# Attention into a bilinear FFN on one core: the ring of attention outputs 2048 columns long instead of 2304

## The chip, the core and the metric

The kernel runs on one core of a Trainium2 chip. The metric is the device time of one execution in microseconds; a lower number is better. The core's engines are called as the profile calls them: PE is TensorE (matmuls; PEld are its weight loads), DVE is VectorE, ACT is ScalarE, POOL is GpSimd and SP is SyncE. They run side by side, each through its own list of instructions in order, and wait for one another through semaphores.

## What is computed

The reference is a sparse attention, whose output is the input of a bilinear feed-forward layer:

```python
batch, n_heads, seq, head_dim = (8, 8, 576, 64)
...
scores = scale * np.matmul(q, k.transpose(0, 1, 3, 2))
mask_local = (rel >= 0) & (rel < stride)                                  # heads 0 to 3, stride 32
mask_strided = (rel >= 0) & (pos[None, :] % stride == pos[:, None] % stride)   # heads 4 to 7
...
attn = attn / (np.sum(attn, axis=-1, keepdims=True) + 1e-09)
...
x = np.ascontiguousarray(attn_out.transpose(0, 2, 1, 3)).reshape(B * S, H * D)   # 4608 x 512
a = x @ w_a          # 512 x 1536
b = x @ w_b          # 512 x 1536
return (a * b @ w_out).astype(np.float32)     # 4608 x 512
```

## The kernel before

**The two halves and what joins them.** There are 8 batches of 576 tokens, 4608 tokens in all. The attention works by batch, the feed-forward layer by tiles of 512 tokens (TTOK), nine of them (0 to 8). They are joined by `xT`, a bf16 tile of 128 partitions, 4 blocks of 128 channels (KD), and a ring of columns, one for each token. The ring is XR = 4 batches, 2304 columns long. Token n lies in column n mod 2304.

**Writing the ring.** For batches 0 and 1 ScalarE copies transposed blocks into it (X_e). For batches 2 to 7 `step_VT` does it. A batch has eight units u = 0 to 7: channel block c = u // 2, half = u % 2; blocks 0 and 1 hold the local heads, 2 and 3 the strided ones. One unit is: S (scores into a PSUM tile `st`, Exp on ScalarE, L391, and the mask on VectorE, L401), and some slots later V. V is matmuls into the PSUM tile `o` (L484), ScalarE's Ln and Exp of the sums (L493, L494), which give their reciprocal, and two VectorE products of `o` with it, one for each head j, into partitions 0 to 63 and 64 to 127 of `xT` (L498 for local heads, L500 for strided). A local half is 288 tokens in a row. A strided half is 4 tokens of each 8 of the whole batch. There is one buffer of `o`, so the matmuls of V wait for the products of the V before.

**Reading the ring.** `ab_mm` (L578) computes the projections of a tile: 12 blocks f of 128 hidden channels, for each of the two weights 4 matmuls of 512 columns, one for each channel block, into one PSUM bank. Tile 4 holds tokens 2048 to 2559, which lie in columns 2048 to 2303 and 0 to 255. So its matmuls are cut in two, of 256 columns each, by the list `cuts`; every piece loads its weights again. ScalarE copies bank a into `a_sb` (L595), VectorE multiplies it with bank b into `pf` (L598; L600 in tiles 0 and 1).

**The second product.** Tiles 2 to 8 (FAST_Y) compute it by seven half-size products, in the order 3, 4, 1, 7, 5, 2, 6 (L683). Their operands are sums of parts of `pf`, which VectorE makes as `ps` (fast_s: L611, L613, L615). VectorE also adds some of the products' banks (L659, L662, L664, L672), ScalarE copies others, GpSimd subtracts (listed under L874), and SP stores the result.

**The order of the work.** It is written out by hand. A tile is 16 slots, 12 of projections and 4 of the second product. The dictionary LATER puts the units of batch b at positions counted from slot 16(b - 1): V0 at 1, V1 at 3, V2 at 5, V3 at 7, V4 at 9, V5 at 11, V6 at 12.5, V7 at 14. So batch b is written during tile b - 1: batch 3 during tile 2, batch 7 during tile 6. In the same slots VectorE transposes the q and k of later batches (L326, L331), which POOL's queue has loaded, and SP's queue moves the transposed blocks. L929 is a one-element GpSimd instruction that keeps POOL's queue in step with the slots.

Of the kernel before, what the change touches and what calls it, by code (L numbers as in the profile page):

```python
# [8 lines left out]
BF16 = mybir.dt.bfloat16  # L9
# [7 lines left out]
RS = 8  # L17
NP = 72
# [12 lines left out]
def kernel(  # L31
# [10 lines left out]
    nc = tc.nc  # L42
    B, H, S, D = q.shape
# [5 lines left out]
    KD = d_model // 128  # L49
    FD = d_ff // 128  # L50
    TTOK = 512
    NT = n_tok // TTOK
    HL = H // 2
    W = S // 2

    const = ctx.enter_context(tc.tile_pool(name="const", bufs=1))
# [97 lines left out]
                             rhs=nc.const_aps.tensor(1.0, [128, 224], BF16), start=True, stop=True)  # L154

    cur = {}
    XR = 4
    xT = const.tile([128, KD, XR * S], BF16)
    wa_sb = wp.tile([128, KD, d_ff], BF16)
    wb_sb = wp.tile([128, KD, d_ff], BF16)  # L160
    wo_sb = wp.tile([128, FD, d_model], BF16)
# [200 lines left out]
    def unit(u):  # L362

        c, half = u // 2, u % 2
        return (c, half, 128, LW, 3) if c < 2 else (c, half, NP, NP, 4)
# [85 lines left out]
    def V_n(b, u):  # L451
        c, half, M, n, G = unit(u)
        ov, _ = held.pop((b, "o", u))
        rc = held.pop((b, "rc", u))
        if (b, c // 2) not in xn:
            x = sb.tile([128, RS * 4 * D], BF16, tag="xr", name="xr", bufs=2)
            xn[b, c // 2] = x[:n, :S // n * 4 * D].rearrange("p (g h d) -> p g h d", h=4, d=D)
        x = xn[b, c // 2][:, :, 2 * (c % 2):2 * (c % 2) + 2, :]
        if c < 2 or b >= FIRST_D:
            dst = x[:, G * half:G * half + G].rearrange("p g j d -> p j g d")  # L460
        else:
            dst = x[:, :, half, :].rearrange("p (g j) d -> p j g d", j=2)
        nc.vector.tensor_mul(dst, ov, rc[:n, :, :G].unsqueeze(3).to_broadcast([n, 2, G, D]))

    def step_V(b, u):
        if b >= FIRST_D:
            step_VT(b, u)
            return
        V_p(b, u)
        V_r(b, u)  # L470
        V_n(b, u)

    def step_VT(b, u):

        c, half, M, n, G = unit(u)
        p = ps.pop((b, u))
        o = psum4["o"].tile([128, 2, 512], F32, tag="o", name="o")
        for i in range(G):
            for j in range(2):
                if c < 2:  # L480
                    vt = vl_buf[b % 2][:, (2 * c + j) * 6 + 3 * half + i]
                else:
                    vt = vs_buf[b % 2][:, 2 * (c - 2) + j, 4 * half + i]
                nc.tensor.matmul(o[:, j, i * n:(i + 1) * n], lhsT=vt, rhs=p[:M, j, i * n:(i + 1) * n], start=True, stop=True)  # L484

        r = sb.tile([128, RS * 4 * D], BF16, tag="xr", name="xr", bufs=2)[:64, :4 * W].bitcast(F32)
        r = r.rearrange("p (j w) -> p j w", j=2)
        if c < 2:
            sums = o[64:, :, :W]
        else:  # L490

            sums, r = (t.rearrange(e, p=NP) for t, e in ((o[64:, :, :W], "d j (g p) -> d j p g"), (r, "d j (p g) -> d j p g")))
        nc.scalar.activation(r, sums, ACT.Ln)  # L493
        nc.scalar.activation(r, r, ACT.Exp, scale=-1.0)  # L494
        for j in range(2):
            dst = xT[64 * j:64 * j + 64, c, S * (b % XR):S * (b % XR + 1)]
            if c < 2:
                nc.vector.tensor_mul(dst[:, W * half:W * (half + 1)], o[:64, j, :W], r[:, j])  # L498
            else:
                nc.vector.tensor_mul(dst.rearrange("d (p r) -> d p r", r=RS)[:, :, G * half:G * (half + 1)],  # L500
                                     o[:64, j, :W].rearrange("d (g p) -> d p g", p=NP), r[:, j])

    def X_p(b, c):
        x = xn[b, c // 2][:, :, 2 * (c % 2):2 * (c % 2) + 2, :]
# [7 lines left out]
    def X_e(b, c):  # L512
        n = LW if c < 2 else NP
        tp = held.pop((b, "x", c))
        tv = tp.rearrange("d (g p) -> d g p", p=n)
        dst = xT[:, c, S * (b % XR):S * (b % XR + 1)]
        if c >= 2:
            dst, tv = dst.rearrange("d (p r) -> d p r", r=RS), tv.rearrange("d g p -> d p g")
        else:
            tv = tp  # L520
        nc.scalar.copy(dst, tv)

    def step_X(b, c):
        X_p(b, c)
        X_e(b, c)

    PART = {"Tkp": lambda c: T_p(0, c, "k"), "Tke": lambda c: T_e(0, c, "k"), "Tqp": lambda c: T_p(0, c, "q"),
            "Tqe": lambda c: T_e(0, c, "q"), "Sp": lambda u: S_p(0, u), "Sx": lambda u: S_x(0, u),
            "Sm": lambda u: S_m(0, u), "Vp": lambda u: V_p(0, u), "Vr": lambda u: V_r(0, u), "Vn": lambda u: V_n(0, u),
            "Xp": lambda c: X_p(0, c), "Xe": lambda c: X_e(0, c)}  # L530

    ORDER = """
# [34 lines left out]
        return psum4[nm].tile(shape, F32, tag=nm, name="mm")  # L567

    def ab_mm(t, f, ab, kks, mid=None, first=0, last=KD - 1):
        n = min(TTOK, XR * S - TTOK * t % (XR * S))  # L570
        cuts = [(0, n)] + ([(n, TTOK - n)] if n < TTOK else [])
        for w, ps_ in zip((wa_sb, wb_sb), ab):
            if mid and ps_ is ab[1]:
                mid()
            for kk in kks:
                for c0, n in cuts:
                    x0 = (TTOK * t + c0) % (XR * S)
                    nc.tensor.matmul(ps_[:, c0:c0 + n], lhsT=w[:, kk, 128 * f:128 * (f + 1)], rhs=xT[:, kk, x0:x0 + n],  # L578
                                     start=(kk == first and c0 == 0), stop=(kk == last and c0 == cuts[-1][0]))

    def ffn_ab(t, f, mid, ab=None):
        if f == 0:
            pfs[t] = fsb.tile([128, FD, TTOK], BF16, tag="pf", name="pf", bufs=1)
        pf = pfs[t]
        if ab is None:
            ab = [mm_bank([128, TTOK]) for _ in range(2)]
            if f == 0:

                late = 1 if t == 1 else 3
                ab_mm(t, f, ab, [kk for kk in range(KD) if kk != late], last=-1)  # L590
                ab_mm(t, f, ab, [late], first=-1, last=late)
            else:
                ab_mm(t, f, ab, range(KD), mid)
        a_sb = fsb.tile([128, TTOK], F32, tag="a_sb", name="a_sb")
        nc.scalar.copy(a_sb, ab[0])  # L595
        if t in FAST_Y:
            halves = lambda x: x.rearrange("p (a i s) -> p a i s", i=2, s=16)
            nc.vector.tensor_mul(pf[:, f, :].rearrange("p (i a s) -> p a i s", i=2, s=16), halves(a_sb), halves(ab[1]))  # L598
        else:
            nc.vector.tensor_mul(pf[:, f, :], a_sb, ab[1])  # L600
        return pf[:1, f, :1]
# [192 lines left out]
    with tc.manual_schedule(engines={ENG.PE, ENG.SP, ENG.Pool, ENG.DVE, ENG.Activation}):  # L794
# [28 lines left out]
        first = {}  # L823
        for nm in ORDER:
            if nm[0] == "*":
                spin(int(nm[1:]))
            elif nm == "C0":
                for x, cp, n in ((raw[0], nc.vector.tensor_copy, "k"), (raw[1], nc.scalar.copy, "q")):
                    t = nats[0, n, False][:, 0:2].rearrange("p h r d -> p (h r d)")
# [21 lines left out]
            elif nm[0] == "F":  # L851
                f = int(nm[1])
# [110 lines left out]
```

## Time and profile before

| | |
|---|---|
| median of the runs shown | 329.73 us (329.67 to 330.11, 4 runs) |
| the profiled execution, its own time | 329.77 us |
| its span (first to last instruction) | 327.6 us |
| granted TensorE clock, mean of the span | 0.998 |
| projections, L578, 512 columns | 727 matmuls in the record, 379 ns each from start to end |
| projections, L578, 256 columns (tile 4) | 192 matmuls, 273 ns each |
| weight loads of the projections, L578 | 960, 98 ns each |
| products into the ring, L498 | 48 of 64 x 288, 447 ns each |
| products into the ring, L500 | 48 of 64 x 288, 448 ns each |

A row of the profile's groups names the line, the engine and the operation, the tile written and the tiles read, the shape, the number of instructions, the busy time in us and the mean of one in ns. In the timeline a row begins with the start and the duration in us; neighbours of one kind are merged ("x4"), and the duration then goes from the first start to the last end. The matmuls are pipelined: one begins before the one ahead has ended, so their pace is the distance of the starts. Some records of matmuls are missing (727 of 768 of the first kind are there).

### The profile page before, as it was taken

Reading aid. Unit: us, or ns where it says so; the run is one execution under the profiler, and the core shown is the slowest. Engines: PE = TensorE matmul, PEld = TensorE weight load, DVE = VectorE, ACT = ScalarE, POOL = GpSimd, SP = SyncE. Lnnn points to the kernel's source line nnn. Section 1 sums busy time; section 2 is a strip of 40 time slices with the busy share of each in tenths; the row PEclk is TensorE's granted clock in tenths of the full one; section 3 lists DMA queues with packets and bytes.
Section 4 is the critical chain, followed back from the end, with each engine's and each line's share of the span. In section 5 each row is a group of like instructions: output and inputs, shape, how many; then the busy total and the mean of one; then the engine's idle time right before and its main releaser. Section 6 shows DMA issues by size and latency. Waiting matters only on the chain.

```text
span 327.6 us, 7651 instructions
## 1 busy us (share of the span) xinstructions
PE 320.7 (98%) x2793; PEld 206.0 (63%) x2824; DVE 265.5 (81%) x509; ACT 201.1 (61%) x325; POOL 177.2 (54%) x296
## 2 busy tenths in 40 slices
PE   8999999999999999999999999999999999999995
PEld 6754555455555577557999985559555954584474
DVE  6767787889777999999999999999877945647662
ACT  5763676468777775876577757776777543313321
POOL 8945938887956665775577557844312131232021
PEclk9999999999999999999999999999999999999999
DMA  9999999799999599899998999898024022004004
GB/s 155 145 204 201 204 184 184 159 180 120 140 205 114 96 94 82 75 211 132 79 87 169 159 88 75 143 204 85 20 63 128 2 67 64 0 2 128 1 2 128
DMA packets 98870, 37.50 MB, mean 114 GB/s; under 512 B 76689, under 2 KB 96017, under 8 KB 98833
## 3 DMA queue, kind: packets, MB, share of 16 engines
q0 software_dynamic: 85968, 19.48, 66.5%
q1 hardware_dynamic: 12576, 17.34, 18.3%
q8 instruction: 22, 0.36, 0.4%
q10 hardware_dynamic: 288, 0.20, 0.2%
q14 instruction: 16, 0.12, 0.1%
HBM read 39.51 MB, written 9.44 MB: 149 GB/s over the span
## 4 chain that ended last, share of the span: by engine, by line
PE 88%; DMA 4%; POOL 4%; issue 1%; DVE 1%; ACT 0%; POOLq 0%; DVEq 0%
PE mm L578 53%; PE mm L683 17%; PE mm L765 6%; PE st L383 4%; DMA wb_sb<-in_moe_w_b_dram 4%; PE o L484 4%; PE mm L711 2%; POOL shared L196 1%; POOL vl L224 1%; POOL wa_sb L251 1%; PE end L711 1%; PE o L440 0%; POOL wb_sb L251 0%; POOL tk L237 0%; PE tp L509 0%
## 5 line engine op out<-in xcount | busy, mean ns | idle before, releaser
L578 PE MATMUL mm<-xT,wb_sb 128*128 128x512 bf16 (+1 forms) x468 | 109.6, 358 | 0.2
L578 PE MATMUL mm<-xT,wa_sb 128*128 128x512 bf16 (+1 forms) x451 | 108.8, 357 | 1.0
L595 ACT COPY a_sb<-mm 128x512 f32<-128x512 f32 x106 | 62.0, 585 | 49.1 <-PE mm L578 47.8
L929 POOL CAST pace<-pf 1x1 f32<-1x1 bf16 x84 | 31.3, 372 | 83.8 <-DVE pf L598 81.0
L578 PEld LDWEIGHTS <-wb_sb 128*128 128x128 bf16 x480 | 46.1, 98 | 44.9 <-DMA wb_sb<-in_moe_w_b_dram 1.2
L598 DVE TENSOR_TENSOR pf<-a_sb,mm 128x512 bf16<-128x512 f32 x84 | 56.4, 671 | 17.0 <-PE mm L578 13.8
L578 PEld LDWEIGHTS <-wa_sb 128*128 128x128 bf16 x480 | 42.6, 98 | 31.4
L391 ACT ACTIVATE p<-st 128x576 bf16<-128x576 f32 (+1 forms) x64 | 41.5, 649 | 12.8 <-PE st L383 11.9
L493 ACT ACTIVATE xr<-o 64x576 f32<-64x576 f32 x48 | 31.1, 647 | 25.1 <-PE o L484 24.2
L683 PEld LDWEIGHTS <-ps 128*128 128x128 bf16 x360 | 34.6, 98 | 3.9
L494 ACT ACTIVATE xr<-xr 64x576 f32<-64x576 f32 x48 | 32.8, 683 | 1.5
L498 DVE TENSOR_TENSOR xT<-o,xr 64x288 bf16<-64x288 f32 x48 | 21.5, 447 | 7.7 <-ACT xr L494 7.1
L500 DVE TENSOR_TENSOR xT<-o,xr 64x288 bf16<-64x288 f32 x48 | 21.5, 448 | 6.4 <-ACT xr L494 5.1
L683 PE MATMUL mm<-wf,ps 128*128 128x256 bf16 x216 | 26.4, 273 | 0.0
L401 DVE TENSOR_TENSOR p<-p,mask_l 128x576 int16<-128x576 int16 x32 | 22.2, 692 | 1.3 <-ACT p L391 1.3
L765 PE MATMUL mm<-wo_sb,pf 128*128 128x512 bf16 x91 | 22.8, 379 | 0.3
L242 POOL DMA_DIRECT2D vs<-in_v_dram x24 | 19.6, 818 | 3.4 <-PE st L383 2.2
L600 DVE TENSOR_TENSOR pf<-a_sb,mm 128x512 bf16<-128x512 f32 x22 | 14.8, 673 | 5.3 <-ACT a_sb L595 3.7
L211 POOL DMA_DIRECT2D ql<-in_q_dram x24 | 16.0, 666 | 5.2 <-DMA wo_sb<-in_moe_w_out_dram 4.1
L211 POOL DMA_DIRECT2D kl<-in_k_dram x24 | 16.1, 671 | 4.8 <-issue 4.0
L929 POOL COPY pace<-y_sb 1x1 f32<-1x1 f32 x16 | 2.8, 175 | 28.8 <-ACT y_sb L666 15.0
L683 PE MATMUL mm<-wf,pf 128*128 128x256 bf16 x144 | 17.6, 273 | 0.0
(160 smaller groups left out, 503.8 us busy)
## 6 DMA issues: line engine op xcount, KB each, us to landing
out_dram<-y_sb SPq DMA_DIRECT2D x12, 512.0 KB, 4.8
out_dram<-y_sb SPq DMA_DIRECT2D x10, 256.0 KB, 3.7
vl<-in_v_dram POOLq DMA_DIRECT2D x6, 384.0 KB, 6.9
kl<-in_k_dram POOLq DMA_DIRECT2D x24, 72.0 KB, 3.1
ql<-in_q_dram POOLq DMA_DIRECT2D x24, 72.0 KB, 3.3
vs<-in_v_dram POOLq DMA_DIRECT2D x24, 72.0 KB, 4.0
wo_sb<-in_moe_w_out_dram POOLq DMA_DIRECT2D x4, 384.0 KB, 9.1
natk<-in_k_dram POOLq DMA_DIRECT2D x20, 72.0 KB, 3.4
```

Source lines behind the costliest of these rows:

```text
L211: nc.gpsimd.dma_start(out=t[32 * h:32 * h + 32], in_=src[b, h].rearrange("(i y) d -> y i d", y=32))
L391: nc.scalar.activation(p[:M, :, :W], st[:M, :, :W], ACT.Exp, scale=scale)
L401: nc.vector.tensor_tensor(pi, pi, mk, op=ALU.bitwise_and)
L493: nc.scalar.activation(r, sums, ACT.Ln)
L494: nc.scalar.activation(r, r, ACT.Exp, scale=-1.0)
L498: nc.vector.tensor_mul(dst[:, W * half:W * (half + 1)], o[:64, j, :W], r[:, j])
L578: nc.tensor.matmul(ps_[:, c0:c0 + n], lhsT=w[:, kk, 128 * f:128 * (f + 1)], rhs=xT[:, kk, x0:x0 + n], start=(kk == first and c0 == 0), sto ...
L595: nc.scalar.copy(a_sb, ab[0])
L598: nc.vector.tensor_mul(pf[:, f, :].rearrange("p (i a s) -> p a i s", i=2, s=16), halves(a_sb), halves(ab[1]))
L683: nc.tensor.matmul(bank[b][:, q], lhsT=lhs(g, q), rhs=rhs(g), start=new and q == 0 and g == 0, stop=g == FG - 1, skip_group_check=True)
L765: nc.tensor.matmul(ybank[j], lhsT=pf[:, f, 128 * j:128 * (j + 1)], rhs=wo_sb[:, f], start=(f == 0), stop=(f == FD - 1))
L929: nc.gpsimd.tensor_copy(pace, done)
```

## The change

The ring becomes XC = 4 x 512 = 2048 columns long. A tile's 512 tokens now always lie in one piece, so `ab_mm` loses its cuts, and tile 4 reads columns 0 to 511. Batches 3 (tokens 1728 to 2303) and 7 (tokens 4032 to 4607) now run over the end of the ring. The new function `x_parts` gives one or two pieces (column, first token, end token), and `step_VT` writes each with an instruction of its own; a strided half is cut along its positions. X_e writes batches 0 and 1 to the same columns as before.

```diff
-    XR = 4
-    xT = const.tile([128, KD, XR * S], BF16)
+    XC = 4 * TTOK
+    xT = const.tile([128, KD, XC], BF16)
...
+    def x_parts(b, t0, t1):
+        x0 = (S * b + t0) % XC
+        e = t0 + XC - x0
+        return ((x0, t0, e), (0, e, t1)) if e < t1 else ((x0, t0, t1),)
...
         for j in range(2):
-            dst = xT[64 * j:64 * j + 64, c, S * (b % XR):S * (b % XR + 1)]
+            x = xT[64 * j:64 * j + 64, c]
             if c < 2:
-                nc.vector.tensor_mul(dst[:, W * half:W * (half + 1)], o[:64, j, :W], r[:, j])
+                for x0, t0, t1 in x_parts(b, W * half, W * (half + 1)):
+                    nc.vector.tensor_mul(x[:, x0:x0 + t1 - t0], o[:64, j, t0 - W * half:t1 - W * half],
+                                         r[:, j, t0 - W * half:t1 - W * half])
             else:
-                nc.vector.tensor_mul(dst.rearrange("d (p r) -> d p r", r=RS)[:, :, G * half:G * (half + 1)],
-                                     o[:64, j, :W].rearrange("d (g p) -> d p g", p=NP), r[:, j])
+                for x0, t0, t1 in x_parts(b, 0, S):
+                    ps_ = slice(t0 // RS, t1 // RS)
+                    dst = x[:, x0:x0 + t1 - t0].rearrange("d (p r) -> d p r", r=RS)
+                    nc.vector.tensor_mul(dst[:, :, G * half:G * (half + 1)],
+                                         o[:64, j, :W].rearrange("d (g p) -> d p g", p=NP)[:, ps_], r[:, j, ps_])
...
-        dst = xT[:, c, S * (b % XR):S * (b % XR + 1)]
+        dst = xT[:, c, S * b:S * (b + 1)]
...
-        n = min(TTOK, XR * S - TTOK * t % (XR * S))
-        cuts = [(0, n)] + ([(n, TTOK - n)] if n < TTOK else [])
+        x0 = TTOK * t % XC
         for w, ps_ in zip((wa_sb, wb_sb), ab):
             if mid and ps_ is ab[1]:
                 mid()
             for kk in kks:
-                for c0, n in cuts:
-                    x0 = (TTOK * t + c0) % (XR * S)
-                    nc.tensor.matmul(ps_[:, c0:c0 + n], lhsT=w[:, kk, 128 * f:128 * (f + 1)], rhs=xT[:, kk, x0:x0 + n],
-                                     start=(kk == first and c0 == 0), stop=(kk == last and c0 == cuts[-1][0]))
+                nc.tensor.matmul(ps_, lhsT=w[:, kk, 128 * f:128 * (f + 1)], rhs=xT[:, kk, x0:x0 + TTOK],
+                                 start=kk == first, stop=kk == last)
```

## The prediction, made before the changed kernel was run

> **What bounds the kernel now.** I read the page first, then a table of the tiles, then TensorE's and VectorE's timelines around the places that the change touches. All durations are of the one profiled execution: 329.77 us, of which its span is 327.6 and 2.17 lies around it. The median of the runs shown is 329.73, so what is added to 329.77 can be added to the median.
>
> ```profile
> PE 320.7 (98%) x2793; PEld 206.0 (63%) x2824; DVE 265.5 (81%) x509; ACT 201.1 (61%) x325; POOL 177.2 (54%) x296
> ...
> PE 88%; DMA 4%; POOL 4%; issue 1%; DVE 1%; ACT 0%; POOLq 0%; DVEq 0%
> ```
>
> TensorE is busy 98% of the span and carries 88% of the chain that ended last. The clock row of the page is 9 in every slice. So a microsecond taken from TensorE's stream counts in full, provided that nobody else is late. The busy times of five tiles (2 to 6, each cut from its first projection to that of the next) say who could be:
>
> ```profile
> core 0: us, PE busy (x) PEld busy (x) DVE busy (x) ACT busy (x) POOL busy (x), PEclk, DMA share, GB/s
> 93.69:127.71 34.03, 33.87 (x293) 21.70 (x294) 30.93 (x57) 25.01 (x41) 20.07 (x36) 1.00 0.95 117
> 127.71:161.74 34.02, 33.81 (x292) 21.70 (x294) 33.51 (x58) 24.52 (x39) 22.92 (x39) 1.00 0.98 125
> 161.74:196.00 34.27, 34.27 (x392) 31.09 (x390) 33.39 (x57) 24.51 (x39) 22.74 (x38) 1.00 0.95 123
> 196.00:230.03 34.02, 33.82 (x292) 21.70 (x294) 33.29 (x57) 24.52 (x39) 21.40 (x37) 1.00 0.96 123
> 230.03:263.80 33.77, 33.56 (x286) 21.45 (x288) 27.60 (x51) 24.51 (x39) 6.98 (x12) 1.00 0.18 52
> ```
>
> Tile 4 (third row) has some 100 matmuls more than its neighbours, yet lasts only 0.24 us longer. VectorE is nearly full in tiles 2 to 5 and has room only in tile 6. No wait of TensorE is listed in any of these tiles: both engines are full, and TensorE leads by a little.
>
> **What goes: tile 4's second pieces.** Each of its 24 groups (12 blocks, two weights) is 8 matmuls of 256 columns now and becomes 4 of 512. TensorE's timeline shows one group of each kind; a group's pace is the distance to the next group's start:
>
> ```profile
> 133.66 1.03 PE L578 MATMUL mm<-xT,wa_sb 128*128 128x512 bf16 x4
> 134.52 1.03 PE L578 MATMUL mm<-xT,wb_sb 128*128 128x512 bf16 x4
> ...
> 167.74 1.04 PE L578 MATMUL mm<-xT,wa_sb 128*128 128x256 bf16 x8
> 168.61 1.04 PE L578 MATMUL mm<-xT,wb_sb 128*128 128x256 bf16 x8
> ```
>
> That is 0.86 us whole and 0.87 cut. By single starts in the trace the steps are 215.6 ns and 109.2 ns, so a group saves 8 x 109.2 - 4 x 215.6 = 11 ns, and 24 groups 0.27 us. The tile table, which contains everything else too, gives 34.27 - 34.02 = 0.24 (34.266 against 34.025 by starts). I take **-0.24**. The 96 weight loads that go too last 98 ns each, but lie beside the matmuls: they are worth nothing by themselves. Even if all of it is won, the kernel is 0.07% faster.
>
> **What comes: VectorE parts.** Batch 3 occupies ring columns 1728 to 2304, so it is cut at its token 320; batch 7 starts at column 1984 and is cut at its token 64. A V step writes two halves of the partitions, one instruction each (L498 for local heads, L500 for strided). Batch 3: V1 and V3 (32 + 256 columns) and V4 to V7 (160 + 128) are cut; V0 and V2 end before the cut. Batch 7: V0 and V2 (64 + 224) and V4 to V7 (32 + 256). Each cut step has 4 instructions for 2, so 12 more per batch, 24 in all. The columns stay the same; each new instruction costs only its fixed part, e.
>
> The trace has no second part of such a write. Bounds for e: it is not below 0, as the same columns are streamed. Full-partition adds of the same kind start one after another 0.60 us apart at 512 columns (L659 at 123.26, next 123.86), 0.34 at 256 (L718), 0.21 at 128 (L739): 1.03 ns a column and 0.07 us over. These start about 0.08 us before the instruction ahead has ended. The pair of an L500 does not: its second starts 0.46 us after its first, which took 0.45. That is 0.16 over the columns. So **e is 0.07 or 0.16**. What differs in the pair is that the output moves from partitions 0-63 to 64-127; the instruction after the pair, back on partition 0, is also spaced so, while the first of the pair is not. A new part writes the same partitions as the one ahead of it. I take 0.07, the nearest row, and keep 0.16 as the other end.
>
> [...]
>
> **Who waits for the parts in tile 2 (batch 3).** VectorE's timeline, from V4 on:
>
> ```profile
> 115.11 0.91 DVE L500 TENSOR_TENSOR xT<-o,xr 64x288 bf16<-64x288 f32 x2
> ...
> 119.00 0.69 DVE L611 TENSOR_TENSOR ps<-pf 128x1024 bf16<-128x1024 bf16 x1
> 119.61 0.91 DVE L500 TENSOR_TENSOR xT<-o,xr 64x288 bf16<-64x288 f32 x2
> ...
> 122.16 1.18 DVE L613 TENSOR_TENSOR ps<-pf 128x2048 bf16<-128x2048 bf16 x1
> 123.26 0.68 DVE L659 TENSOR_TENSOR ya<-mm,ya 128x512 f32<-128x512 f32 x1
> 123.86 0.90 DVE L500 TENSOR_TENSOR xT<-o,xr 64x288 bf16<-64x288 f32 x2
> ```
>
> V4's write (115.11) starts 0.03 after ScalarE's Exp and 0.12 after VectorE's last end: it keeps time with TensorE. From there to V6's write VectorE never rests. Behind it stand two weight loads, seen in narrow windows of the timeline:
>
> ```profile
> 123.39 0.10 PEld L683 LDWEIGHTS <-ps 128*128 128x128 bf16 x1
> ```
> ```profile
> 124.81 0.10 PEld L484 LDWEIGHTS <-vs 72*128 72x128 bf16 x1
> ```
>
> The first belongs to product 5 and reads the sums of L613, which ended at 123.33; it starts 0.05 later, 122 ns after the load ahead, where 109 is the rule of the stream. The second starts 0.05 after V6's write ended (124.76): V7's o reuses that PSUM buffer. Both loads are already released by VectorE, with nothing to spare; their matmuls are just in time. Any delay of VectorE after V4 thus becomes a TensorE stall of the same size.
>
> With e = 0.07 a cut step adds 0.14. V1: 0.14, and V2 follows 0.45 of slack (0.37 idle plus the usual 0.08 of early start): nothing left. V3: 0.14 into V4's 0.20 (0.12 + 0.08): nothing left. V4 + V5: 0.28, all at L613: stall 0.28. V6: 0.14 more at the second load. **Sum for tile 2: +0.42.** V7 starts again in time with Exp; its 0.14 runs into the mask L401 of tile 3 (128.98 to 131.23, 2.25 us for 0.45 elsewhere). That mask ends 0.33 after a GpSimd add (129.62 + 1.28), as those of tiles 4 and 5 do, so it ends no later if it starts 0.14 later: nothing. Without that cover 0.14 - 0.07 of slack at V4 of tile 3 would reach the same load there (157.41): +0.07.
>
> Tile 6 (batch 7): VectorE idles 0.77 to 0.89 ahead of V0 to V4. V4's 0.14 goes into the 0.06 + 0.08 ahead of V5's write, V5's into the 0.20 idle ahead of L401; L613 ends 0.86 before its load. V6's o has 0.87 to V7, V7 idles 1.24 first. **0.**
>
> **Waits of the shorter ring: 0.** Batch 4's columns were read by tiles 0 and 1, batch 7's by tiles 3 and 4 (done at 185.8, first write 235.6). Tile 4's last operand, V7 of batch 4, ends at 161.71; the matmuls on it start at 163.04. POOL and SP get no instruction and no DMA more.
>
> **Sum:** -0.24 + 0.42 = +0.18, so 329.77 + 0.18 = 329.95 by the profiled run, 329.9 by the median.
>
> **Rivals.** 0.2% is 0.66 us, about what a measurement of this kernel can tell from no change.
> 1. *Slower: the parts do not overlap*, e = 0.16, 0.32 a step. V3 leaves 0.32 - 0.20 = 0.12, V4 to V6 add 0.96: 1.08 of stall in tile 2, -0.24: +0.84, 330.6. It passes 0.66 from 8e - 0.20 - 0.24 = 0.66, e = 0.14. For: every L498 and L500 pair. Against: all neighbours on one partition start.
> 2. *The cover is better than read*: the loads have room or the parts cost next to nothing, and only -0.24 is left: 329.5. Against: the 122 ns.
> 3. *No gain in tile 4*, VectorE holding it at 34.27: +0.42, 330.2. Against: tiles 3 and 5 do the same VectorE work in 34.02.
>
> **Chances.** Forecast with rival 3 (about 329.75 to 330.25) 0.55; rival 2 0.15; rival 1 0.22, 0.04 of it under 0.66; something unseen, a shifted GpSimd or DMA collision, 0.08, half either way. Faster 0.04, within 0.2% 0.74, slower 0.18 + 0.04 = 0.22. The range takes in rivals 1 and 2: 329.45 to 330.65.
>
> **What would show it.** Tile 4 at 34.03. Part to part 0.24 us at 160 columns says e = 0.07, over 0.3 says 0.16. A gap of TensorE ahead of product 5 and of V7 in tile 2, together 0.4; tile 2 at 34.45. Tiles 3, 5 and 6 unchanged. Wrong if tile 2 stays at 34.03 or tile 6 grows.

## The result and the profile after

The changed kernel takes 330.13 us (median of 34 runs) against 329.80 (55 runs of the kernel before, beside them): ratio 1.0011, 95% interval 1.0006 to 1.0017, that is +0.36 us with an interval of 0.2 to 0.56. (The ratio is not simply the quotient of the two medians, here and below.) The prediction said +0.18 and "within 0.2%". The profiled execution took 330.42 us with a span of 327.9.

The page of the changed kernel, the same two lines as of before:

```profile
PE 320.3 (98%) x2693; PEld 196.9 (60%) x2728; DVE 267.0 (81%) x533; ACT 201.2 (61%) x325; POOL 177.5 (54%) x296
...
PE 92%; POOL 2%; DMA 2%; issue 1%; DVE 1%; POOLq 0%; ACT 0%; DVEq 0%
```

PEld has 96 instructions less, DVE 24 more (509 to 533), as counted. TensorE is the bound as before. The five tiles, cut from first projection to first projection (columns as in the prediction):

```profile
93.95:128.28 34.33, 34.17 (x293) 21.55 (x294) 31.62 (x69) 25.00 (x41) 20.17 (x36) 1.00 0.94 112
128.28:162.30 34.02, 33.82 (x292) 21.70 (x294) 33.46 (x58) 24.51 (x39) 22.89 (x39) 1.00 0.98 124
162.30:196.33 34.02, 33.82 (x292) 21.69 (x294) 33.30 (x57) 24.51 (x39) 22.74 (x38) 1.00 0.97 124
196.33:230.36 34.03, 33.82 (x292) 21.69 (x294) 33.30 (x57) 24.51 (x39) 21.43 (x37) 1.00 0.96 123
230.36:264.13 33.77, 33.56 (x286) 21.46 (x288) 28.16 (x63) 24.51 (x39) 6.98 (x12) 1.00 0.19 52
```

Only two rows moved. Tile 2 went from 34.03 to 34.33 with 12 VectorE instructions more (x57 to x69), tile 4 from 34.27 to 34.02 with 96 matmuls less (100 in the records, which miss some). Tile 6 got its 12 instructions too (x51 to x63) and lasts 33.77 as before. By the starts in the trace (tile 2 34.026 to 34.333, tile 4 34.266 to 34.025) that is +0.307 and -0.241: +0.07 in all.

VectorE in tile 2 from V4's write to V6's, where the timeline of before had pairs of 0.91 and 0.90:

```profile
115.38 1.04 DVE L510 TENSOR_TENSOR xT<-o,xr 64x160 bf16<-64x160 f32 x4
...
119.39 0.69 DVE L618 TENSOR_TENSOR ps<-pf 128x1024 bf16<-128x1024 bf16 x1
120.00 1.03 DVE L510 TENSOR_TENSOR xT<-o,xr 64x160 bf16<-64x160 f32 x4
...
122.67 1.18 DVE L620 TENSOR_TENSOR ps<-pf 128x2048 bf16<-128x2048 bf16 x1
123.78 0.68 DVE L666 TENSOR_TENSOR ya<-mm,ya 128x512 f32<-128x512 f32 x1
124.38 1.02 DVE L510 TENSOR_TENSOR xT<-o,xr 64x160 bf16<-64x160 f32 x4
```

Four parts take 0.12 to 0.13 more than two whole writes did. The two weight loads that stood right behind VectorE (L613 of before is L620 here, L484 is L489), each in a narrow window of the timeline:

```profile
123.91 0.10 PEld L690 LDWEIGHTS <-ps 128*128 128x128 bf16 x1 [0.28 <-DVE ps L620]
```
```profile
125.45 0.10 PEld L489 LDWEIGHTS <-vs 72*128 72x128 bf16 x1 [0.23 <-DVE xT L510]
```

Both now wait visibly: the bracket is the load engine's idle time and who ended it. The matmuls show it too. First the three around the first load, before and after, then the ones behind the second load:

```profile
123.26 0.49 PE L683 MATMUL mm<-wo_sb,ps 128*128 128x256 bf16 x3
```
```profile
123.52 0.67 PE L690 MATMUL mm<-wo_sb,ps 128*128 128x256 bf16 x3
...
125.46 0.24 PE L489 MATMUL o<-p,vs 72*128 72x72 bf16 x2
```

TensorE's matmul stream has a gap of 0.168 us at the first and of 0.118 at the second (distance of the starts less the usual step), and no other one between 93 and 240 us (steps that are one missing record longer are left out). The 0.02 that is left of the 0.307 lies in the steps right behind the two gaps.

So the tiles explain +0.07 of the measured +0.36. The two profiled executions differ by 0.65 (329.77 and 330.42), and what is not in the tiles lies in two places. The first projection of tile 1 starts at 58.17 and 58.44, and the time outside the span (execution less span) is 2.14 and 2.49 (the prediction's 2.17 goes by the rounded span). From tile 8 on the changed kernel's execution is 0.03 shorter. Whether the later start belongs to the change is a question for the experiments; the time outside the span is taken up behind them.

### The profile page after: what moved, and what is told of

It is laid out like the page before. It is cut to its first block, busy times and chain, and to the rows that moved or that the text cites. A ratio compares the mean times of both kernels' runs of the same rounds, so it can differ in the third digit from the quotient of the medians.

```text
span 327.9 us, 7480 instructions
## 1 busy us (share of the span) xinstructions
PE 320.3 (98%) x2693; PEld 196.9 (60%) x2728; DVE 267.0 (81%) x533; ACT 201.2 (61%) x325; POOL 177.5 (54%) x296
## 4 chain that ended last, share of the span: by engine, by line
PE 92%; POOL 2%; DMA 2%; issue 1%; DVE 1%; POOLq 0%; ACT 0%; DVEq 0%
PE mm L585 55%; PE mm L690 17%; PE mm L772 6%; PE st L383 5%; PE o L489 4%; DMA vl<-in_v_dram 2%; PE mm L718 2%; POOL shared L196 1%; PE o L440 1%; PE ab L585 1%; PE tp L519 1%; PE end L718 1%; POOL vl L224 0%; PE tp L286 0%; PE tp L295 0%
## 5 line engine op out<-in xcount | busy, mean ns | idle before, releaser
L585 PE MATMUL mm<-xT,wa_sb 128*128 128x512 bf16 x400 | 108.5, 379 | 1.2
L585 PE MATMUL mm<-xT,wb_sb 128*128 128x512 bf16 x419 | 109.3, 379 | 0.2
L585 PEld LDWEIGHTS <-wb_sb 128*128 128x128 bf16 x432 | 41.7, 98 | 48.9
L585 PEld LDWEIGHTS <-wa_sb 128*128 128x128 bf16 x432 | 37.9, 98 | 33.4
L504 DVE TENSOR_TENSOR xT<-o,xr 64x288 bf16<-64x288 f32 (+4 forms) x56 | 22.0, 403 | 7.2 <-ACT xr L499 6.5
L510 DVE TENSOR_TENSOR xT<-o,xr 64x288 bf16<-64x288 f32 (+2 forms) x64 | 22.5, 371 | 5.9 <-ACT xr L499 4.8
L690 PE MATMUL mm<-wo_sb,ps 128*128 128x256 bf16 x144 | 17.7, 273 | 0.0
```

The lines of the kernel that those rows point to most:

```text
L510: nc.vector.tensor_mul(dst[:, :, G * half:G * (half + 1)], o[:64, j, :W].rearrange("d (g p) -> d p g", p=NP)[:, ps_], r[:, j, ps_])
L585: nc.tensor.matmul(ps_, lhsT=w[:, kk, 128 * f:128 * (f + 1)], rhs=xT[:, kk, x0:x0 + TTOK], start=kk == first, stop=kk == last)
L690: nc.tensor.matmul(bank[b][:, q], lhsT=lhs(g, q), rhs=rhs(g), start=new and q == 0 and g == 0, stop=g == FG - 1, skip_group_check=True)
```

## The experiments

Theory A: the change is what the tiles show, and the start phase varies by itself. Theory B: the change also lengthens the start phase, for instance by the addresses of all tiles that lie behind the ring.

**Each half alone.** e1 puts the cuts into the kernel before; `x_parts` is called as in the changed kernel:

```diff
+    def x_parts(b, t0, t1):
+        x0 = S * (b % XR)
+        e = {3: 320, 7: 64}.get(b, 0)
+        return ((x0 + t0, t0, e), (x0 + e, e, t1)) if t0 < e < t1 else ((x0 + t0, t0, t1),)
```

> The kernel before (ring of 2304, tile 4 still in 256-column pieces) with only the writes of batches 3 and 7 cut at the same tokens as in the changed kernel. Theory A (the changed kernel is what its tiles show: tile 2 +0.31 us from the cut writes, tile 4 -0.24 us, nothing elsewhere that belongs to the change): tile 2 at 34.33, tile 4 at 34.27, the others as before, +0.31 us against the kernel before. Theory B (part of the measured +0.33 us comes from elsewhere in the change, such as the 0.26 us that the profiled run lost ahead of tile 1, for instance through the addresses of all tiles behind the shortened ring): the tiles as in A, and also +0.31, since the ring's size is that of before; told apart from A by the run with a padded ring only. Rival C (the cut writes are hidden): 0.

Measured: 330.52 us against 329.91, ratio 1.0015 (1.0007 to 1.0024). Tiles 2 to 4:

```profile
93.39:127.74 34.35, 34.34 (x297) 21.58 (x294) 31.64 (x69) 25.03 (x41) 20.23 (x36) 1.00 0.96 117
127.74:161.76 34.02, 34.02 (x296) 21.70 (x294) 33.50 (x58) 24.54 (x39) 22.97 (x39) 1.00 0.97 124
161.76:196.03 34.27, 34.27 (x393) 31.13 (x390) 33.41 (x57) 24.55 (x39) 22.78 (x38) 1.00 0.97 123
```

The cuts cost 0.32 us in tile 2 and nothing in tiles 3 and 6 (33.77). Rival C, cuts that are hidden, is out. The ratio says +0.49 us (0.23 to 0.79), more than the tile; see the time outside the span below.

e2 is the other half, whole matmuls without a cut write:

```diff
-        cuts = [(0, n)] + ([(n, TTOK - n)] if n < TTOK else [])
+        cuts = [(0, TTOK)]
...
-                    x0 = (TTOK * t + c0) % (XR * S)
+                    x0 = min(TTOK * t % (XR * S), XR * S - TTOK)
```

> The kernel before with the ring of 2304 and no cut write, and only tile 4's projections in whole 512-column matmuls; to be able to do so they read columns 1792 to 2303, so tile 4 is computed from the wrong tokens. Theory A and B: tile 4 at 34.03, all other tiles as before, -0.24 us. Rival (VectorE holds tile 4 at 34.27): 0.

Measured: 329.43 against 329.91, ratio 0.9990 (0.9981 to 1.0000). Tiles 2 to 4:

```profile
93.34:127.37 34.03, 34.03 (x297) 21.73 (x295) 30.94 (x57) 25.04 (x41) 20.12 (x36) 1.00 0.96 115
127.37:161.39 34.02, 34.02 (x296) 21.70 (x294) 33.52 (x58) 24.55 (x39) 22.96 (x39) 1.00 0.97 124
161.39:195.41 34.02, 34.02 (x296) 21.69 (x294) 33.31 (x57) 24.53 (x39) 22.79 (x38) 1.00 0.99 124
```

Tile 4 gains its 0.24 in full. VectorE, busy 33.3 us, does not hold it back. By reading other columns e2 also spares tile 4 its wait for batch 4's writes; that is not where the gain comes from, since the changed kernel keeps this wait and its tile 4 takes the same 34.02.

**What a part costs.** e3 only changes the order of the parts:

```diff
-        for j in range(2):
+        for (x0, t0, t1), j in [(part, j) for part in (x_parts(b, W * half, W * (half + 1)) if c < 2 else x_parts(b, 0, S)) for j in range(2)]:
             x = xT[64 * j:64 * j + 64, c]
```

> The changed kernel with the four parts of a cut write in another order: first part for head 0, first part for head 1, second part for head 0, second part for head 1, so that each instruction writes another half of the partitions than the one ahead. If an instruction that moves to another half starts only after the one ahead has ended (14 ns after, as the pairs of before), a cut step costs 0.31 us over a whole one instead of 0.13: V3 leaves 0.31 - 0.20 = 0.11, V4 and V5 add 0.62, 0.10 of it is covered by a weight load that can lie beside its matmul, V6 adds 0.31: tile 2 at 34.03 + 0.94 = 34.97, +0.70 us against the kernel before. If the order doesn't matter: tile 2 at 34.33, +0.07 us.

Measured: 331.21 against 329.91, ratio 1.0033 (1.0021 to 1.0045). Tiles 2 to 4, then V4's write and the next instruction on VectorE, then who TensorE's weight loads waited for in tile 2 from 106 us on (us in total, times, longest):

```profile
93.88:129.10 35.22, 34.72 (x297) 21.37 (x295) 32.38 (x68) 25.03 (x41) 20.43 (x36) 1.00 0.94 109
129.10:163.12 34.02, 34.02 (x296) 21.72 (x294) 33.46 (x59) 24.53 (x39) 22.97 (x39) 1.00 0.97 123
163.12:197.15 34.03, 34.03 (x297) 21.70 (x295) 33.32 (x57) 24.53 (x39) 22.78 (x38) 1.00 0.98 124
```
```profile
115.60 1.23 DVE L510 TENSOR_TENSOR xT<-o,xr 64x160 bf16<-64x160 f32 x4
116.86 0.78 DVE L326 STREAM_TRANSPOSE tq<-ql 128x576 bf16<-128x576 bf16 x1
```
```profile
PEld L690 <- DVE ps L620: 0.6, 1, 0.6
PEld L489 <- DVE xT L510: 0.4, 1, 0.4
PEld L383 <- DMA qz11s<-tq: 0.3, 1, 0.3
PEld L690 <- DVE pf L605: 0.2, 1, 0.2
```

The same instructions in another order cost 0.31 more a step than whole writes (from V4's first start to the next instruction 1.26 us; 1.07 in the changed kernel; 0.95 before). A second part of the same half starts 0.24 us after a first of 160 columns; a part of the other half starts 0.32 after it, 14 ns after its end. Tile 2 is 1.19 longer than before, not 0.94: its gaps are 0.12 at the load of `pf`, 0.06 at V6's matmuls, 0.51 and 0.32 at the two loads, together 1.00, and 0.16 more at 107.5 us, where a load waits for a DMA of q. No other profiled run has that one, so I count it to this run and not to the order, though with one profile of e3 that is not shown. The mechanism is the one that was expected; its size is 1.0 for 0.94.

**Room for VectorE.** e4 moves one transpose of tile 2 from ahead of L620 to behind V6's write:

```diff
-            gs = {2: (14, 14, 15, 15, 16, 16, 17, 17, 18, 18), 3: (8, 9, 10, 11, 12, 13, 14, 15, 16, 17)}.get(b) or (
+            gs = {2: (14, 14, 15, 15, 16, 16, 17, 17, 18, 18), 3: (8, 9, 10, 11, 12, 13, 14, 15, 16, 17),
+                  4: (3, 5, 7, 9, 13, 13, 14, 15, 16, 17)}.get(b) or (
```

> The changed kernel with one VectorE transpose (0.63 us) of tile 2 moved from ahead of the sums L620 to behind V6's write. If VectorE's chain from V4 to V6 is what stalls TensorE in tile 2, both stalls go: tile 2 at 34.03, tile 4 at 34.03, -0.24 us against the kernel before. V7's write and the add behind it are then some 0.5 us later, with 0.64 of room ahead of tile 3, and a mask that ends with a GpSimd add anyway. Rival (the late transpose only moves the stall to the start of tile 3): tile 3 up to 0.3 longer, about +0.07.

Measured: 329.57 against 329.91, ratio 0.9989 (0.9977 to 1.0001). Tiles 2 to 4:

```profile
93.97:128.00 34.03, 34.03 (x297) 21.73 (x295) 31.30 (x68) 25.01 (x41) 20.19 (x36) 1.00 0.97 117
128.00:162.02 34.02, 34.02 (x297) 21.71 (x294) 33.51 (x59) 24.51 (x39) 22.93 (x39) 1.00 0.97 124
162.02:196.05 34.03, 34.03 (x297) 21.73 (x295) 33.31 (x57) 24.51 (x39) 22.73 (x38) 1.00 0.99 124
```

Both stalls are gone with all 24 parts still there, and tile 3 pays nothing. So within the tiles the parts cost time only because of VectorE's chain in front of the two loads. By the tiles this version is 0.24 us below the kernel before.

**The start phase.** The kernel before and the changed one once more, and the changed one with the ring padded, so that nothing behind it moves:

```diff
-    xT = const.tile([128, KD, XC], BF16)
+    xT = const.tile([128, KD, 4 * S], BF16)
```

> The kernel before itself, once more, as a control for the others of this call. 0 against the kernel before; tiles 2 and 4 at 34.03 and 34.27. Its start phase (first instruction to the first projection of tile 1, 58.17 us in the profiled run of before, 58.44 in that of the changed kernel) is one more sample: if it varies by some tenths from run to run of one kernel, the 0.26 us between those two runs is no property of the change.

> The changed kernel itself, once more. Theory A (its excess is tile 2 +0.31 and tile 4 -0.24, the rest of the measured +0.33 us is the varying start phase): +0.07 us against the kernel before, within an interval of some 0.3. Theory B (the change also lengthens the start phase): +0.33 again, and a start phase of 58.4 against 57.8 to 58.2 of kernels with the ring of before.

> The changed kernel with the ring's tile still 2304 columns wide, of which it uses 2048, so that every tile behind it keeps the address that it has in the kernel before. Theory A: as the changed kernel, tile 2 at 34.33, tile 4 at 34.03, +0.07 us. Theory B with the addresses as its cause: the start phase is that of before, and the time is 0.26 us below that of the changed kernel in the same call.

Measured, against 329.82 for the kernel before beside them: r1 329.82, ratio 1.0004 (0.9994 to 1.0014); r2 330.03, 1.0005 (0.9996 to 1.0014); r3 330.20, 1.0010 (0.9998 to 1.0023). The padded ring is not faster. The two gaps of tile 2 repeat in e1, r2 and r3 (0.17 to 0.18 and 0.125 us) and are absent from r1, as from e2 and e4. Last, e4 again and e4 with the padded ring:

> The changed kernel with the later transpose of e4 and with the padded ring of r3. Theory A: as e4, tile 2 and tile 4 at 34.03, -0.24 us against the kernel before, whatever the padding. Theory B (addresses behind the shortened ring lengthen the start phase by some 0.3 us): a start phase of 57.7 to 58.3 against 58.4 of the unpadded one in this call, and 0.3 us below it.

> The kernel of e4 itself once more, beside its padded form. Theory A: -0.24 us against the kernel before, the same as e5. Theory B: 0.3 us above e5, with a start phase of 58.4.

Measured, again against 329.82: e5 329.73, ratio 1.0006 (0.9996 to 1.0016); r4 329.77, ratio 0.9998 (0.9988 to 1.0008). In both, tiles 2 and 4 are 34.03 again. The start of tile 1 in all eleven profiled executions:

| ring's tile | kernel, start of tile 1 (us) |
|---|---|
| 2304 columns | before 58.17, r1 58.29, e1 57.88, e2 57.83, r3 57.74, e5 57.97 |
| 2048 columns | after 58.44, r2 58.10, e3 58.37, e4 58.46, r4 57.77 |

One and the same program differs from run to run by 0.34 (after and r2) and 0.69 (e4 and r4), more than the 0.26 in question. Theory B, which wanted 58.4 in r4 and 0.3 less in e5, is not borne out. But theory A is not the whole either: its +0.07 lies just under the interval of the first comparison (0.2 to 0.56), although it lies within that of r2 (-0.13 to 0.46).

**The time outside the span.** For every execution of the changed kernel and of the experiments, and of the kernel before beside these, the time and the span are on record. Their difference is what lies ahead of the first instruction and behind the last; single values are good to 0.05 us, since the spans are rounded to 0.1.

| kernel | cut writes | executions on record | time less span, mean (lowest to highest), us |
|---|---|---|---|
| before, beside the experiments, and r1 | no | 92 | 2.15 (2.09 to 2.22) |
| e2 | no | 12 | 2.14 (2.10 to 2.18) |
| after | yes | 35 | 2.37 (2.15 to 2.54) |
| r2 (after again) | yes | 12 | 2.29 (2.17 to 2.45) |
| r3 (padded ring) | yes | 12 | 2.36 (2.13 to 2.54) |
| e1 (ring of 2304) | yes | 12 | 2.36 (2.15 to 2.49) |
| e3 | yes | 5 | 2.39 (2.26 to 2.43) |
| e4, e5, r4 (later transpose) | yes | 34 | 2.24 (2.19 to 2.28) |

Every kernel with the cut writes takes longer here, whatever the length of its ring, and e2, without them, does not. So about 0.2 us of the difference belongs to the change after all, but it lies neither in the tiles nor in the start phase. The tiles and this time together make +0.29 for the changed kernel, +0.22 for r2 and +0.53 for e1; the measured +0.36, +0.16 and +0.49 have these sums in their intervals. The span itself grows no more than its tiles: its mean is 327.79 in r2 and 327.74 in the kernel before beside it, each good to about 0.1. For the version with the later transpose the two make -0.15. The intervals of e4 (-0.76 to 0.03) and r4 (-0.40 to 0.26) hold that, the one of e5 (-0.13 to 0.53) just misses it, and none of the three shows by the measured time that this version is faster than the kernel before.

What takes this time is not shown, nor why it is less with the later transpose. The traces have one hint. In the profiled executions of after, r2, e1 and e3 (2.31 to 2.49 us outside the span) a second transfer of 8 KB on q14, a queue of the kind "instruction", begins 2.24 to 2.28 us behind the last instruction. The other seven (2.14 to 2.22) have only one transfer there, 0.97 to 1.29 behind it; four of these seven have the cut writes as well.

## Why the prediction was right, step by step

- **Tile 4, -0.24.** Measured -0.241, by itself in e2 too. Rival 3, VectorE holding the tile, fell.
- **The price of a part, e = 0.07.** A cut step cost 0.12 to 0.13 for 0.14, so e is 0.06 to 0.065. Rival 1's 0.16 is what the same parts cost when they alternate (e3, 0.31 a step): the choice of the nearest row was the one that mattered. With e = 0.16 the second part on the same half was to start over 0.3 us after a first of 160 columns; it starts 0.24 after it, 0.075 us before the record of the first ends.
- **Who waits, +0.42.** The two loads named are the only places that stall, and e4 shows that VectorE's chain ahead of them is the reason. The size was 0.307. The term that failed is the first stall, 0.28: L620 did end 0.26 later against TensorE's stream, but the stall was 0.17. The step said that the load had "nothing to spare" and any delay "becomes a TensorE stall of the same size". The load had none, but its matmul had: it started 5 ns after its delayed load had started (123.905 and 123.910), while before the same load started 95 ns ahead of its matmul (123.385 and 123.480; 108 ns in the undisturbed stream). So 0.09 us of the delay was covered. With that lead counted, the step would have put the first stall at 0.19 instead of 0.28. At the second load the cover had been used up by the delay it already carried, and V6's own 0.12 came through as 0.118.
- **V1, V3, V7 and tile 6: nothing.** Tiles 3 and 6 are unchanged. V7's four parts end later, and the mask behind them still ends with the GpSimd add. The changed kernel's GpSimd and VectorE rows around the start of tile 3 (128.28):

```profile
129.61 2.12 DVE L401 TENSOR_TENSOR p<-p,mask_l 128x576 int16<-128x576 int16 x1
130.13 1.27 POOL L881 TENSOR_TENSOR y_sb<-ye,y_sb 128x512 f32<-128x512 f32 x1
```

  It ends 0.33 after the add, as before, 3.45 us into the tile (3.51 before).
- **The sum.** +0.07 by the tiles for +0.18; the measured times say +0.36 (0.2 to 0.56). The sum lies just below that interval, the range (329.45 to 330.65) holds the median, and the change is within 0.2% of no change, as forecast. The nearness of 0.18 to 0.36 is luck in part: tile 2 cost 0.11 less than forecast, and the time outside the span, which the prediction took over from the kernel before as it was, grew by some 0.2 that no term of the sum stands for.

## What to carry to other kernels

Work moved here from the bounding engine to another one was paid for where the other engine was the last to arrive. In this kernel such places are weight loads that start 0.05 us after an instruction of that engine; the new work to count is what lies between there and the last point at which that engine was idle, less the lead that the load has on its matmul (0.095 us at the first of them). Twelve parts cost 0.31 us in tile 2, where VectorE had no rest, and nothing once one transpose had been moved behind the deadline; the twelve of tile 6, where VectorE idles up to 0.9 us ahead of a write, cost nothing. When a write must be cut, keep the parts on the same partitions next to each other (1.07 us for such a step here, 1.26 with the parts alternating). And compare the time outside the span as well: here it held a larger part of the difference than all tiles together.

## What the runs showed of the hardware that was not expected

- A matmul whose weight load was late started 5 ns after the load had started; the load took 98 ns, and that matmul 284 ns instead of 273. In the changed kernel some 0.09 us of such a delay was covered at each of the two loads: the first was 0.26 late and the stall 0.17, the second 0.20 late against the stream and the stall 0.12.
- The order of four VectorE writes, nothing else, was worth 0.19 us a step (1.26 against 1.07) and 0.89 us of tile 2 (35.219 against 34.333, with the 0.16 of the DMA wait in it).
- With 24 instructions more on VectorE the time outside the span grew from 2.15 us to 2.29 to 2.39, with one transpose moved besides to 2.24 only. Its cause is open.
- The start phase of one program, up to tile 1, varied by up to 0.69 us between two executions, while tiles 3, 5, 6 and 7 repeat within some 0.003 us in all eleven. Tenths of a microsecond are told from the tiles here, and hardly from the total.
